# Four 32-wide parts of the array for a linear-attention kernel's state and query products, with weighting in halves and a new written-out order

## The chip, the cores and the metric

The kernel runs on one core of a Trainium2 chip. The metric is the device time of one execution in microseconds (us). Five engines run side by side: TensorE (PE: matmuls; PEld: its weight loads), VectorE (DVE), ScalarE (ACT), GpSimd (POOL), and SyncE (SP), which issues nearly all DMAs.

## What is computed

A transformer block on x of 2048 tokens by 640, in bfloat16: a linear attention with 32 heads of 20 on a layer-normalised x, added to x, then a SiLU feed-forward of width 1728 on the layer-normalised sum, added again. The attention is the part that the change touches:

```python
pq = jnp.einsum("bhsd,hdf->bhsf", q, w_phi)
pk = jnp.einsum("bhsd,hdf->bhsf", k, w_phi)
phi_q = jnp.concatenate([_softmax(pq, axis=-1), _softmax(-pq, axis=-1)], axis=-1)
phi_k = jnp.concatenate([_softmax(pk, axis=-1), _softmax(-pk, axis=-1)], axis=-1)
kv = jnp.einsum("bhsf,bhsd->bhfd", phi_k, v)
z  = jnp.einsum("bhsf->bhf", phi_k)
num = jnp.einsum("bhqf,bhfd->bhqd", phi_q, kv)
den = jnp.einsum("bhqf,bhf->bhq", phi_q, z)[..., None] + 1e-6
o = num / den
```

So each head has a state of 2 x 20 rows (sign s = 0 and 1) by 21 columns (20 of v and one of z), summed over all tokens, and each query row is multiplied with it.

## The kernel before

The 2048 tokens are 16 tiles of 128 rows (t); the 640 channels are 5 chunks of 128 (C). The program has no loop of its own: a string ORDER lists some 630 words, each an operation with its arguments, and every engine executes its part of them in that order, each instruction waiting for what it needs. "kp.3.0.1" is op_kp(3, 0, 1).

The stages, with the words and the lines of what they issue:

- **Weights and inputs.** lx, lk, lv, lp, lq, lo, l1, l2, lh load X, the weights of k, v, the features, q, the output and the feed-forward (nearly all on SP's queue). wt, wc, fk, fc fold the k weights with the feature weights (transposes L303, products L318); lq, gk, gc do it for q. wm (L255) are matmuls on a dummy tile `warm` that warm TensorE up, eight of them ahead of the first word.
- **First normalisation.** st (L261) takes the statistics on VectorE, rs and rm the reciprocal root on POOL, xn (L278 on VectorE or L283 on ACT) the normalised tile, xt and xc or xd (a transposing DMA, L296) its transpose.
- **State.** vp and kp (L348) give v and the features of k; vc copies v beside a column of ones; ke (L369) takes both exponentials, kr (L377, L380) their sums and reciprocals, ka or kb (L385) multiplies them in, on POOL ("p" a whole tile, "h" its first half) and VectorE (kb, the second half). cc (L407) adds a tile's part to the state `kv`, 20 matmuls of all 128 rows by 64 columns of the array: for each sign and chunk, two parts of 64 features stand side by side on the array's columns, each with 4 heads of 21 columns (84). km (L417) multiplies the state with a mask that keeps each head's own block, into KVBD.
- **Queries.** qp (L427) gives the q features of four tiles, qe (L437) the exponentials; dp (L460) multiplies a tile's 128 queries with the state, for each sign in 10 matmuls of 64 rows by 128 columns, with 4 heads of 22 columns (88; the last is z). dw weights the two signs (reciprocal L473, product L474, L476, sum L480), dr (L489) takes the reciprocal of the sum, do (L495, half a tile each, POOL or VectorE) divides, td (L515) transposes by DMA.
- **Output and feed-forward.** op (L522) is the output product, oa (L531) adds X, sq (L539), sa and sr (POOL, L544 to L555), hn (L561) and hd (L581, a transposing DMA) are the second normalisation, up (L596, the tail L606) and ua (L618) the first half of the feed-forward in five groups of 2, 4, 4, 4 and 2 tiles, yp, yq (L642) and yh (L657) the second half, yo and yz (L665, L677) the sum, so and sz the stores.

Nearly all products go through one pool `mm` of four PSUM buffers of two banks. A buffer is free for the next product once all its readers are done; the order of the words decides which product gets which buffer. One buffer holds the state from the first cc to km. dp takes two buffers a tile, one for each sign.

The features of the queries are laid out so that chunk r of the array's rows holds features 64r to 64r + 63 of the first 16 heads in its upper half and of the other 16 in its lower; gc (one copy a chunk) puts Wfq into that layout.

Of the kernel before, what the change touches and what calls it, by code (L numbers as in the profile page):

```python
# [25 lines left out]
lp.a lx.2.4.s ta lk.2.3.s lk.0.1.s mk lk.3.4.s lk.1.2.s lk.4.5.s lv.0.3.s ph.p lx.1.2.s st.3  # L26
lx.0.1.s wt.2 lv.3.5.s st.2 wc.2.a rs.3 lx.4.8.s wm.512 wt.0 wm.256 wt.3 wc.0.a fk.2 wc.3.v rs.2
wt.1 fc.2.a fk.0 xn.3.v fk.3 wc.1.v mc fc.0.a xt.3 fk.1 xc.3.v wt.4 fc.1.a xn.2.v wm.256 vp.3.0.3
lq.4 wc.4.v fc.3.a st.1 mo xt.2 kp.3.0.1 lq.0 xc.2.a kp.3.1.2 kp.3.2.3 st.0 fk.4 vp.2.0.3 fc.4.a
lx.8.12.s rs.0.2 lq.3 vp.3.3.5 kp.3.3.4 vc.3.a kp.3.4.5 xn.0.v vp.2.3.5 lq.1 xn.1.v ke.3 st.5  # L30
kp.2.0.1 kp.2.1.2 xt.0 lh.s kp.2.2.3 st.4 xc.0.a kp.2.3.4 xt.1 vc.2.a kp.2.4.5 lq.2 kp.0 st.6 rs.4.2
ke.2 xn.5.v vp.0 xc.1.a xn.4.v xd.5 st.7 ke.0 kp.1 st.11 lx.12.16.s rs.6.2 vc.0.a xd.4 st.8 vp.1
ke.1 xn.7.v st.10 gk.2 xd.7 gk.0 gc.2.a vp.5 st.9 vc.1.a lo.s gc.0.a kr.1 gk.3 rs.8.4 kp.5 gc.3.a
rm.10 gk.1 xn.9.v ke.5 ka.1.p vp.4 st.12 xd.9 gc.1.a st.14 kp.4 vc.5.a xn.8.v vc.4.a rm.6 st.15 xd.8
vp.7 ke.4 st.13 kp.7 xn.6.a kr.2 rs.12.4 xn.10.a xd.6 vp.9 ke.7 rm.13 xn.12.v ka.2.p kr.4 kp.9 xd.12
vc.9.a vc.7.a gk.4 l2.0.4.s ke.9 vp.8 xd.10 xn.14.v ka.4.p kr.0 gc.4.a vp.6 xn.13.a vc.8.a kr.3 kp.6
rm.11 rm.15 ka.0.p cc.2 kr.7 cc.1 ke.6 cc.4 kp.8 ka.3.p vc.6.a kr.5 xn.15.a qp.0.0 ke.8 xd.15 ka.7.p
kr.9 xd.14 vp.12 qe.0.0 l2.8.13.s ka.5.p kr.8 kp.12 l1.1.s vc.12.a xn.11.a qp.1.0 ke.12 ka.8.p xd.11
kr.12 kp.15 l1.0.s qe.1.0 xd.13 ka.9.p kp.10 l1.2.s l2.4.8.s cc.0 cc.7 ka.12.p ke.10 cc.3 cc.5 cc.8
kr.10 vp.10 kp.14 vc.10.a kr.6 ka.10.p ke.15 kp.11 ke.14 kp.13 ka.6.h ke.11 kr.14 vp.15 ke.13 kr.11  # L40
ka.14.p qp.0.2 qp.0.1 qe.0.2 kr.13 vc.15.a ka.11.p vp.13 kr.15 vp.14 ka.13.p vc.13.a qe.0.1 kb.6
vp.11 vc.14.v ka.15.p cc.12 vc.11.a cc.9 cc.6 cc.11 cc.10 cc.14 cc.13 cc.15 qp.1.2 km.0 close km.1
dp.1.0 qe.1.2 dp.1.1 qp.1.1 dw.1.v dp.0.1 qe.1.1 dp.0.0 dr.1 qp.2.1 dw.0.v dp.3.1 qe.2.1 dp.3.0 dr.0
qp.3.0 dw.3.v do.0.0.p do.0.1.p do.1.1.p td.0 dp.5.0 qe.3.0 dp.5.1 dr.3 qp.2.0 dw.5.v do.3.1.p
do.3.0.p do.1.0.p dp.4.1 td.1 qe.2.0 dp.4.0 op.0 dw.4.v td.3 qp.2.2 oa.0 dp.2.1 qe.2.2 dp.2.0 dr.5
sa.0 qp.3.2 dr.4 dw.2.v do.5.1.p sq.0 op.1 do.5.0.p qe.3.2 sr.0 td.5 dp.9.0 dp.9.1 dr.2 qp.3.1 hn.0
do.2.1.p do.2.0.v hd.0 oa.1 do.4.0.p do.4.1.p dw.9.v sq.1 td.2 op.3 sa.1 qe.3.1 sr.1 td.4 op.5 hn.1
dr.9 hd.1 op.2 oa.5 oa.3 sa.5 op.4 do.9.1.p oa.2 up.0.3 sq.2 oa.4 dp.10.1 sa.4 sq.4 dp.10.0 up.0.0
dw.10.v ua.0.3 sr.4 sq.5 sa.3 do.9.0.p dp.6.0 ua.0.0 dp.6.1 up.0.1 sa.2 dw.6.v td.9 sq.3 sr.3 dp.8.1
# [12 lines left out]
sr.14 yp.6.1 sr.11 hn.14 hn.10 hn.12 hd.10 sr.13 yh.2.1 yh.2.0 hd.12 yp.6.0 so.3 hd.14 yp.9.1 yo.6
hn.13 hd.15 yo.8 yp.7.0 hn.11 hd.11 yp.9.0 hd.13 so.6 up.4.0 so.8 yo.9 up.4.3 up.3.1 ua.4.3 yp.7.1
up.3.0 yo.7 ua.3.1 so.7 ua.4.0 so.2 up.4.1 up.3.3 ua.4.1 up.3.6 ua.3.3 up.4.2 ua.3.6 ua.3.0 up.3.4
ua.4.2 up.3.2 ua.3.4 yp.15.0 ua.3.2 up.3.5 yp.14.0 ua.3.5 yp.15.1 yp.10.0 yh.4.0 yh.3.0 yp.12.1
# [5 lines left out]
def kernel(  # L71
# [613 lines left out]
    with tc.manual_schedule(engines={PE, SP, POOL, DVE, ACT}):  # L685
        ps = None
        for i in range(8):
            ps = op_wm(512, ps)
# [30 lines left out]
```

## Time and profile before

| | us |
|---|---|
| median of 3 runs | 239.42 (239.4 to 240.32) |
| the profiled execution | 240.42 |
| its span, from the first to the last instruction | 238.7 |
| TensorE busy, sum | 232.9 |
| VectorE busy, sum | 136.3 |
| ACT busy, sum | 104.8 |
| POOL busy, sum | 88.8 |

A page and its views name groups of instructions by line, engine, operation and tile. A row of the groups gives the shape, the count, the busy time and the mean length of one, and the idle time ahead of them with what ended most of it. A row of the timeline gives start, length, engine, line and count, and in brackets the idle time before it with its releaser. The chain is the work that ended last, followed back from the last instruction; its rows give start and length of each piece. The stretches give for each window the busy us and counts of PE, PEld, DVE, ACT and POOL, then the granted clock of TensorE, the DMA share and GB/s. Matmuls are pipelined: the length of one reaches past the start of the next, so costs are read from start to start. A few matmul records are missing.

### The profile page before, as it was taken

Reading aid. Unit: us, or ns where it says so; the run is one execution under the profiler, and the core shown is the slowest. Engines: PE = TensorE matmul, PEld = TensorE weight load, DVE = VectorE, ACT = ScalarE, POOL = GpSimd, SP = SyncE. Lnnn points to the kernel's source line nnn. Section 1 sums busy time; section 2 is a strip of 40 time slices with the busy share of each in tenths; the row PEclk is TensorE's granted clock in tenths of the full one; section 3 lists DMA queues with packets and bytes.
Section 4 is the critical chain, followed back from the end, with each engine's and each line's share of the span. In section 5 each row is a group of like instructions: output and inputs, shape, how many; then the busy total and the mean of one; then the engine's idle time right before and its main releaser. Section 6 shows DMA issues by size and latency. Waiting matters only on the chain.

```text
span 238.7 us, 5187 instructions
## 1 busy us (share of the span) xinstructions
PE 232.9 (98%) x2143; PEld 150.8 (63%) x2159; DVE 136.3 (57%) x256; ACT 104.8 (44%) x155; POOL 88.8 (37%) x166
## 2 busy tenths in 40 slices
PE   7999999999999999999999999999999999999994
PEld 3777777577584456787655476664566756656762
DVE  3779999938968999889858139623213120000133
ACT  3678897967545674561043620015660014631000
POOL 5722769998870737464101550001424000000000
PEclk9999999999999999999999999999999999999999
DMA  6997945499000136116480004520103701000013
GB/s 204 314 212 168 233 89 140 87 333 312 4 3 3 27 58 110 31 29 58 84 133 7 17 14 82 110 58 0 29 3 83 156 11 55 0 3 0 26 59 110
DMA packets 42807, 20.60 MB, mean 86 GB/s; under 512 B 34336, under 2 KB 42272, under 8 KB 42784
## 3 DMA queue, kind: packets, MB, share of 16 engines
q1 hardware_dynamic: 41984, 20.11, 36.8%
q8 instruction: 17, 0.28, 0.5%
q10 hardware_dynamic: 800, 0.16, 0.4%
q14 instruction: 6, 0.05, 0.1%
HBM read 9.61 MB, written 2.62 MB: 51 GB/s over the span
## 4 chain that ended last, share of the span: by engine, by line
PE 93%; DVE 2%; DMA 2%; issue 1%; ACT 1%; DVEq 0%
PE mm L596 24%; PE mm L642 21%; PE mm L348 18%; PE mm L427 9%; PE mm L522 9%; PE mm L460 3%; PE mm L407 3%; DMA out_dram<-ob 2%; PE mm L255 2%; PE mm L318 1%; PE mm L606 1%; PE mm L657 1%; ACT EqT L437 1%; PE mm L303 1%; DVE xn L278 1%
## 5 line engine op out<-in xcount | busy, mean ns | idle before, releaser
L618 ACT ACTIVATE shT<-mm 128x1024 bf16<-128x1024 f32 (+2 forms) x29 | 27.5, 963 | 77.9 <-PE mm L596 56.2
L596 PE MATMUL mm<-HnT,w 128*128 128x512 bf16 (+1 forms) x316 | 58.7, 335 | 0.5
L642 PE MATMUL mm<-w,shT 128*128 128x320 bf16 (+2 forms) x415 | 58.5, 299 | 0.2 <-issue 0.2
L642 PEld LDWEIGHTS <-shT 128*128 128x128 bf16 x416 | 39.8, 98 | 17.8 <-issue 1.3
L596 PEld LDWEIGHTS <-w 128*128 128x128 bf16 x325 | 31.2, 98 | 23.1 <-issue 0.4
L665 DVE TENSOR_TENSOR ob<-mm,X 128x640 bf16<-128x640 f32 x15 | 12.2, 822 | 46.7 <-PE mm L642 38.3
L348 PEld LDWEIGHTS <-XnT 128*128 128x128 bf16 x320 | 30.8, 98 | 12.3 <-DMA wv<-in_A_wqkv_dram 0.2
L385 POOL TENSOR_TENSOR Ek<-Ek,Sk 128x1280 bf16<-128x1280 bf16 (+1 forms) x16 | 36.9, 2332 | 2.5 <-DVE Sk L380 1.6
L377 DVE TENSOR_REDUCE Sk<-Ek 128x64 f32<-128x1280 bf16 x16 | 23.1, 1445 | 4.5 <-ACT Ek L369 4.5
L437 ACT ACTIVATE EqT<-mm 128x1024 bf16<-128x1024 f32 (+1 forms) x24 | 19.8, 879 | 11.0 <-PE mm L427 11.0
L348 PE MATMUL mm<-Wfk,XnT 128*128 128x320 bf16 x160 | 24.2, 299 | 0.0
L348 PE MATMUL mm<-wv,XnT 128*128 128x320 bf16 x160 | 24.0, 299 | 0.1
L522 PE MATMUL mm<-wo,ot 128*128 128x320 bf16 x160 | 23.8, 299 | 0.0
L427 PE MATMUL mm<-XnT,Wfq 128*128 128x512 bf16 x94 | 23.1, 380 | 0.4
L495 POOL TENSOR_TENSOR o<-u,rd 128x320 bf16<-128x320 f32 x21 | 15.7, 768 | 20.4 <-DVE rd L489 12.0
L531 DVE SCALAR_TENSOR_TENSOR X<-mm,X 128x640 bf16<-128x640 f32 x16 | 12.9, 815 | 17.2 <-PE mm L522 17.2
L369 ACT ACTIVATE Ek<-mm 128x640 bf16<-128x640 f32 x32 | 20.6, 717 | 4.1 <-PE mm L407 3.0
L522 PEld LDWEIGHTS <-ot 128*128 128x128 bf16 x160 | 15.3, 98 | 7.4 <-issue 0.3
L544 POOL TENSOR_SCALAR HM<-HST 128x1 f32<-128x1 f32 x16 | 3.4, 210 | 40.0 <-DVE X L531 40.0
L427 PEld LDWEIGHTS <-Wfq 128*128 128x128 bf16 x100 | 9.2, 97 | 10.2 <-issue 0.3
L261 DVE BATCH_NORM_STATS2 stats<-X 128x6 f32<-128x320 bf16 x32 | 13.6, 467 | 2.7 <-DMA X<-in_A_x_dram 2.7
L561 DVE TENSOR_SCALAR hn<-X,HM 128x640 bf16<-128x640 bf16 x16 | 7.9, 525 | 12.2 <-POOL HM L555 12.2
(71 smaller groups left out, 212.8 us busy)
## 6 DMA issues: line engine op xcount, KB each, us to landing
out_dram<-ob SPq DMA_DIRECT2D x15, 160.0 KB, 2.0
w<-in_B_w_dram SPq DMA_DIRECT2D x3, 720.0 KB, 6.5
X<-in_A_x_dram SPq DMA_DIRECT2D x3, 640.0 KB, 4.9
w<-in_B_w_dram SPq DMA_DIRECT2D x2, 640.0 KB, 6.0
wk<-in_A_wqkv_dram SPq DMA_DIRECT2D x5, 160.0 KB, 3.4
wo<-in_A_wo_dram SPq DMA_DIRECT2D x1, 800.0 KB, 6.7
w<-in_B_w_dram SPq DMA_DIRECT2D x1, 800.0 KB, 5.3
wv<-in_A_wqkv_dram SPq DMA_DIRECT2D x1, 480.0 KB, 5.8
```

Of the source, the lines that this page charges most:

```text
L261: nc.vector.bn_stats(stats[:, k, :], X[:, t, k * 320 : (k + 1) * 320])
L348: nc.tensor.matmul(ps[:, half, 0:320], tok(XnT[t // GT], t)[:, c, :], W[:, c, half * 320 : (half + 1) * 320], start=(c == 0), stop=(c == C ...
L369: nc.scalar.activation(Ek[:, s, :].rearrange("p (a n) -> p a n", a=2), tl["kp", t][:, :, 0:320], AF.Exp, scale=1.0 - 2.0 * s,)
L377: nc.vector.tensor_reduce(Sk[:], tl["ek", t][:].rearrange("p s (h f) -> p (s h) f", f=DH), axis=AX.X, op=ALU.add,)
L385: eng.tensor_tensor(Ek3, Ek3, tl["sk", t][:, lo:hi].unsqueeze(2).to_broadcast([P, hi - lo, DH]), op=ALU.mult,)
L427: nc.tensor.matmul(ps[:, k, :], Wfq[:, c, r * P : (r + 1) * P], XnT[g][:, c, :], start=(c == 0), stop=(c == C - 1),)
L437: nc.scalar.activation(E[:, s, rs[0] : rs[-1] + 1, :], tl["qp", g, i][:, 0 : len(rs), :], AF.Exp, scale=1.0 - 2.0 * s,)
L495: (nc.vector if eng == "v" else nc.gpsimd).tensor_tensor(tl["o", t][:, a * 320 : (a + 1) * 320].rearrange("p (h f) -> p h f", f=DH), tl["u ...
L522: nc.tensor.matmul(ps[:, half, 0:320], tl["ot", t][:, c, :], wo[:, c, half * 320 : (half + 1) * 320], start=(c == 0), stop=(c == C - 1),)
L596: nc.tensor.matmul(ps[:, i * W : (i + 1) * W], w1[:, c, fc * P : (fc + 1) * P], HnT[g][:, c, 0:W], start=(c == 0), stop=(c == C - 1), skip ...
L618: nc.scalar.activation(sh[:, a:b], tl["up", g, k][:, 0 : b - a], AF.Silu)
L642: nc.tensor.matmul(ps, shT[g][:, fc * W + i * P : fc * W + (i + 1) * P], w2[:, fc, a:b], start=first and fc == 0, stop=last and fc == FC - ...
```

## The change

- **State products (cc).** 40 matmuls a tile in place of 20, each 128 rows by 32 columns of the array: four parts of 32 features stand side by side, part g with heads 8g to 8g + 7, and each covers 3 heads of 21 columns (63) in place of 4 (84).
- **Query products (dp).** One word a tile in place of two; 40 matmuls in place of 20, each 32 rows by 128 columns, with 3 heads of 22 columns (66) in place of 4 (88). The four parts write four PSUM banks: one buffer holds both signs of parts 0 and 1, the other those of parts 2 and 3, so each buffer now holds one half x of the heads.
- **Weighting (dw).** dw.t.x does one half of the heads from one buffer: the same four VectorE instructions twice a tile, on half the elements each.
- **Masks and layout.** op_mc makes its mask with 8 selects on 32 rows and 5 copies on POOL, in place of 4 selects; gc copies twice a chunk; km's shapes are smaller.
- **Warm-up.** `warm` is a constant of ones in place of a tile that VectorE fills; nine matmuls ahead of the first word in place of eight; one wm of 512 columns fewer in the order.
- **Order.** All of ORDER is written anew, for all engines. Some words change engine: xn.6, xn.11, xn.15 to VectorE; kb.10 and kb.15 in place of kb.6; nine of the do words, and some copies. The loads of X, wk and the feed-forward weights stand elsewhere in SP's queue; l2.4.8 and l1.2 now stand between the first output transposes; the two last stores swap queues. The lines move: L409 is the state product in the new file, L463 the query product, L479 to L484 the weighting, L521 the output product, L595 and L641 the feed-forward's.

```diff
-    warm = first.tile([P, 512], BF16, name="warm")
-    nc.vector.memset(warm[:], 0.0)
+    warm = nc.const_aps.tensor(1.0, [P, 512], BF16)
...
-                for a in range(2):
-                    q, lo = C * a + r, 64 * a
+                for g in range(4):
+                    lo, q, h = 32 * g, 160 * g + 32 * r, 8 * g + HW[r]
                     nc.tensor.matmul(
-                        kv[s][lo : lo + 64, r, :, :].rearrange("p j c -> p (j c)"),
-                        Ek[:, s, 64 * q : 64 * q + 64],
-                        Vp[:, HQ[q] : HQ[q] + 4, :].rearrange("p h c -> p (h c)"),
+                        kv[s][lo : lo + 32, r, :, :].rearrange("p j c -> p (j c)"),
+                        Ek[:, s, q : q + 32],
+                        Vp[:, h : h + 3, :].rearrange("p h c -> p (h c)"),
...
+    def op_dp(t):
+        G, i = t // GT, t % GT
+        ps = [mm2(), mm2()]
+        for s in range(2):
+            for r in range(C):
+                for g in range(4):
+                    lo, o = 32 * g, 176 * s + 22 * HW[r]
+                    nc.tensor.matmul(
+                        ps[g // 2][:, g % 2, o : o + 66],
+                        EqT[G][lo : lo + 32, s, r, i * P : (i + 1) * P],
+                        KVBD[lo : lo + 32, s, r, :, :].rearrange("p j c -> p (j c)"),
+                        start=(s == 0 and r == 0),
+                        stop=(s == 1 and r == C - 1),
+                        skip_group_check=True,
+                    )
...
+    def op_dw(t, x):
+        A = tl["dp", t][x]
+        if ("u", t) not in tl:
+            tl["u", t] = wk2().tile([P, 2, 2, 8, 21], F32, name="u", bufs=3)
+        u = tl["u", t][:, x]
+        w = sm.tile([P, 2, 8], F32, name="w")
+        nc.vector.reciprocal(w[:], A[:, :, 1, :, 21])
+        nc.vector.tensor_tensor(w[:], w[:], A[:, :, 0, :, 21], op=ALU.mult)
         nc.vector.tensor_tensor(
-            u[:], A[1][:, :, :, 0:21], w[:].unsqueeze(3).to_broadcast([P, 2, 16, 21]), op=ALU.mult,
-        )
...
+            u, A[:, :, 1, :, 0:21], w[:].unsqueeze(3).to_broadcast([P, 2, 8, 21]), op=ALU.mult,
+        )
+        nc.vector.tensor_tensor(u, u, A[:, :, 0, :, 0:21], op=ALU.add)
...
-        for i in range(8):
+        for i in range(9):
             ps = op_wm(512, ps)
```

The new order from the state's end on, up to the sixth output product:

```
... cc.15 cc.11 qp.1.2 km.0 close km.1 dp.1 qe.1.2 qp.1.1 dw.1.1 dw.1.0 dp.0
qe.1.1 dw.0.1 qp.2.1 dw.0.0 dp.3 qe.2.1 dr.1 qp.2.2 dw.3.1 do.1.1.p do.1.0.p qe.2.2 dr.0 dp.4 td.1
dw.3.0 do.0.1.p qp.3.0 do.0.0.p dw.4.0 td.0 op.1 dw.4.1 l2.4.8.s qe.3.0 dr.3 dp.5 oa.1 do.3.0.p
qp.2.0 dr.4 do.3.1.p sq.1 dw.5.0 sa.1 td.3 sr.1 dw.5.1 op.0 qe.2.0 l1.2.s do.4.1.p do.4.0.p qp.3.2
oa.0 td.4 hn.1 dp.2 qe.3.2 dr.5 qp.3.1 dw.2.1 do.5.1.p hd.1 sq.0 do.5.0.p dw.2.0 sa.0 td.5 sr.0
qe.3.1 op.4 dr.2 hn.0 do.2.1.p do.2.0.v dp.9 oa.4 op.5 td.2 dw.9.1 sa.4 sq.4 hd.0 op.3 dw.9.0 op.2
```

And before:

```
... cc.13 cc.15 qp.1.2 km.0 close km.1
dp.1.0 qe.1.2 dp.1.1 qp.1.1 dw.1.v dp.0.1 qe.1.1 dp.0.0 dr.1 qp.2.1 dw.0.v dp.3.1 qe.2.1 dp.3.0 dr.0
qp.3.0 dw.3.v do.0.0.p do.0.1.p do.1.1.p td.0 dp.5.0 qe.3.0 dp.5.1 dr.3 qp.2.0 dw.5.v do.3.1.p
do.3.0.p do.1.0.p dp.4.1 td.1 qe.2.0 dp.4.0 op.0 dw.4.v td.3 qp.2.2 oa.0 dp.2.1 qe.2.2 dp.2.0 dr.5
sa.0 qp.3.2 dr.4 dw.2.v do.5.1.p sq.0 op.1 do.5.0.p qe.3.2 sr.0 td.5 dp.9.0 dp.9.1 dr.2 qp.3.1 hn.0
do.2.1.p do.2.0.v hd.0 oa.1 do.4.0.p do.4.1.p dw.9.v sq.1 td.2 op.3 sa.1 qe.3.1 sr.1 td.4 op.5 hn.1
dr.9 hd.1 op.2 oa.5 oa.3 sa.5 op.4
```

149 lines of the change are left out of this document (60 added, 89 removed).

## The prediction

> **What bounds the kernel now.** I read the page first: the busy shares, and the engines' shares of the chain of work that ended last.
>
> ```profile
> PE 232.9 (98%) x2143; PEld 150.8 (63%) x2159; DVE 136.3 (57%) x256; ACT 104.8 (44%) x155; POOL 88.8 (37%) x166
> PE 93%; DVE 2%; DMA 2%; issue 1%; ACT 1%; DVEq 0%
> ```
>
> TensorE is busy nearly always, and 93% of the chain is its work. A shorter stream of matmuls shortens the kernel, as long as no other engine takes over. Next, the busy times by stretch (PE, PEld, DVE, ACT, POOL), for the stretches where the change lies.
>
> ```profile
> 60.00:80.00 20.00, 19.84 (x300) 12.06 (x302) 16.36 (x25) 10.43 (x14) 11.12 (x6) 1.00 0.01 2
> 80.00:100.00 20.00, 19.83 (x213) 12.00 (x214) 17.88 (x40) 11.23 (x19) 11.08 (x26) 1.00 0.37 66
> 100.00:120.00 20.00, 19.95 (x219) 14.65 (x218) 18.00 (x35) 5.89 (x9) 8.45 (x22) 1.00 0.36 52
> ```
>
> VectorE is busy 18 of 20 us from 80 to 120: in this stage it is the next bound, close behind TensorE. The change gives it more work just there. That is the core of this forecast.
>
> **What a group of small matmuls costs.** The chain's pieces, then TensorE's timeline (start, length, count).
>
> ```profile
> 46.69 2.16 PE mm L427 x10
> 109.19 5.30 PE mm L642 x39
> ```
>
> ```profile
> 67.73 3.30 PE L407 MATMUL mm<-Vp,Ek 128*64 128x84 bf16 x160
> 70.96 1.25 PE L427 MATMUL mm<-XnT,Wfq 128*128 128x512 bf16 x4
> 72.15 0.57 PE L460 MATMUL mm<-KVBD,EqT 64*128 64x88 bf16 x20
> 72.64 2.33 PE L427 MATMUL mm<-XnT,Wfq 128*128 128x512 bf16 x10
> 74.91 0.57 PE L460 MATMUL mm<-KVBD,EqT 64*128 64x88 bf16 x20
> ```
>
> A whole-array matmul takes 216 ns for 512 columns and 136 ns for 320, so 0.417 ns per column plus 2.7 ns. Ten of them fill 2.16 us from 72.64 to 74.80, and the next group starts at 74.91: entering another shape of the array costs about 0.1 us. Leaving costs as much: 20 small matmuls from 72.15 are followed at 72.64, 0.49 us later. With 0.1 us taken off, ten pairs take 0.39 us, about 40 ns a pair; 80 pairs of L407 take 3.23 - 0.1 us, 39.1 ns a pair. One matmul alone would take 37.7 ns (84 columns) or 39.4 ns (88). So the two halves do run together, and a second part costs at most 1.5 ns.
>
> After the change four parts of 63 (state) or 66 (query) columns stand in place of two. If each added part costs 1.5 ns, a group of four takes 28.9 + 4.5 = 33.4 ns or 30.2 + 4.5 = 34.7 ns; if none does, 29 and 30 ns. I take 33 and 34, the value from the pairs.
> - State products: 160 groups x (39.1 - 33) = **-1.0 us** (bounds -1.6 from 29 ns, and +6.2 from the supply of instructions, below).
> - Query products: 10 groups a tile x (40 - 34) = -0.06 us a tile. The first seven tiles lie in a stretch that I find bound by VectorE and are counted there; nine remain: **-0.5 us** (bounds -0.9 and +3.5).
> - Order: yh.1.0 stands alone, one entry and one leaving more, and dp.7 to yh.0.0 and dp.14 to yh.1.1 are no longer of one shape: **+0.3 us** (0 to +0.4).
>
> The supply is the operation that no row shows. A group of four needs 8 instructions (loads and matmuls) in 33 ns, 4 ns each; in the run of 160 each of 320 came in 9.8 ns. If that were the limit, a group would take 78 ns. The pairs fit their columns so well that I take the columns as what bounds them.
>
> [...]
>
> **Weighting in halves (VectorE).** The groups by shape: count, busy us, mean ns.
>
> ```profile
> L476 DVE TENSOR_TENSOR u<-mm,w 128x672 f32<-128x672 f32 x16 | 13.7, 857 | 1.3 <-ACT EqT L437 0.3
> L480 DVE TENSOR_TENSOR u<-u,mm 128x672 f32<-128x672 f32 x16 | 13.7, 854 | 0.6
> L473 DVE RECIPROCAL w<-mm 128x32 f32<-128x32 f32 x16 | 5.4, 339 | 4.8 <-PE mm L460 4.7
> L474 DVE TENSOR_TENSOR w<-w,mm 128x32 f32<-128x32 f32 x16 | 3.0, 188 | 1.0
> L489 DVE RECIPROCAL rd<-u 128x32 f32<-128x32 f32 x16 | 5.3, 343 | 0.2
> L380 DVE RECIPROCAL Sk<-Sk 128x64 f32<-128x64 f32 x16 | 8.8, 553 | 0.6
> L677 DVE TENSOR_TENSOR ob<-mm,X 128x512 bf16<-128x512 f32 x1 | 0.7, 691 | 1.2 <-DMA out_dram<-ob 1.2
> L677 DVE TENSOR_TENSOR ob<-mm,X 128x128 bf16<-128x128 f32 x1 | 0.3, 292 | 0.0
> ```
>
> The two L677 rows give 1.04 ns per element and 159 ns fixed; for 672 elements that is 858, and the row says 857. A half, 336 elements, takes 508 ns, not 428. A reciprocal costs 6.6 ns per element (553 - 343 over 32): 234 for 16. The small product takes 171. A half is 234 + 171 + 2 x 508 = 1.42 us, a tile 2.84 instead of 2.24: **+0.6 us a tile**, 9.6 us in all (bounds 0, if nothing is fixed, and +0.9, if the gaps between dependent instructions double too). Before 80 us TensorE cannot run far ahead of it, because each tile's two buffers of products stay taken until its halves are weighted, and the buffers are four.
>
> Now VectorE's timeline from the state's end to op.2, the output product that in the new order closes the first six.
>
> ```profile
> 71.08 1.10 DVE L417 TENSOR_TENSOR KVBD<-mm,maskS 128x420 bf16<-128x420 f32 x2 [2.15 <-PE mm L407]
> ...
> 90.04 0.45 DVE L561 TENSOR_SCALAR hn<-X,HM 128x640 bf16<-128x640 bf16 x1
> 90.40 1.02 DVE L495 TENSOR_TENSOR o<-u,rd 128x320 bf16<-128x320 f32 x1
> 91.34 0.81 DVE L531 SCALAR_TENSOR_TENSOR X<-mm,X 128x640 bf16<-128x640 f32 x1
> 92.08 0.08 DVE L531 DVE_READ_ACCUMULATOR X<-mm,X 128x1 f32 x1
> ```
>
> ```profile
> 92.21 5.71 PE L522 MATMUL mm<-wo,ot 128*128 128x320 bf16 x40
> 97.76 0.71 PE L596 MATMUL mm<-HnT,w 128*128 128x256 bf16 x5
> ```
>
> ```profile
> ot<-o SPq DMA_TRANSPOSE x16, 2.6
> ```
>
> Before, do.2.0 (the row at 90.40) ends at 91.42, 20.3 us after L417 began; in it lie dw and dr of six tiles, oa.0 and hn.0. After, the same six tiles stand ahead of it, and oa.1 and hn.1 too (0.74 and 0.36 us from start to start in these rows), and L417 is shorter by 2 x 105 elements x 1.04 = 0.2. That is 20.3 + 6 x 0.6 + 1.1 - 0.2 = 24.8 us. The transpose of tile 2 lands 2.6 us after its issue, which takes some 0.2; op.2 starts at 27.6 and ends 1.36 later, at 29.0. Before, the same TensorE work (seven dp, all qp, six op) ended at 97.76 - 71.08 = 26.7. So TensorE waits here, first for buffers, then for VectorE's last result through POOL and the transpose: **+2.2 us** net of the shorter products (0 to +3.5). Behind op.2 on TensorE stand up.0 and everything later. From there nothing is as tight: VectorE waits for dp.10, the next tile, and catches up.
>
> **Warm-up and start.** The chain's first pieces, the timelines of TensorE and of SP, and one row of the page's DMA issues.
>
> ```profile
> 4.84 0.58 PE mm L303 x5
> ```
>
> ```profile
> 9.64 0.97 PE L348 MATMUL mm<-wv,XnT 128*128 128x320 bf16 x6
> 11.09 0.45 PE L289 MATMUL mm<-ident,xn 128*128 128x128 bf16 x5 [0.48 <-DVE xn L278]
> 11.48 0.97 PE L348 MATMUL mm<-Wfk,XnT 128*128 128x320 bf16 x6
> ```
>
> ```profile
> 3.60 0.44 SPq L221 DMA_DIRECT2D wv<-in_A_wqkv_dram  x1
> 4.21 0.84 SPq L221 DMA_DIRECT2D X<-in_A_x_dram  x2
> ```
>
> ```profile
> wv<-in_A_wqkv_dram SPq DMA_DIRECT2D x1, 480.0 KB, 5.8
> ```
>
> The constant lets TensorE start before VectorE's memset; the ninth warm-up fills that time, so the first transposes stay near 4.8. At 11.48 the old order has done five wt, four fk, two xt and vp.3.0.3, with a wait for xn ahead of the row at 11.09. The new order does both xt before its first vp, which waits for wv: 3.60 + 5.8 = 9.4, plus some 0.4 for the one more X load issued ahead of it. From 9.9, with 6 x 0.136 us, it is as far at 10.7: **-0.8 us** (-1.2 to +0.5). op_mc's 8 selects instead of 4 lie in POOL's wait for the row statistics; uncovered they cost about 2 us to xn.0 and xn.1.
>
> **Normalising, on POOL.** The timeline, then the groups by shape.
>
> ```profile
> 60.53 9.88 POOL L385 TENSOR_TENSOR Ek<-Ek,Sk 128x1280 bf16<-128x1280 bf16 x4 [1.13 <-DVE Sk L380]
> ```
>
> ```profile
> L385 POOL TENSOR_TENSOR Ek<-Ek,Sk 128x1280 bf16<-128x1280 bf16 x15 | 35.6, 2403 | 2.5 <-DVE Sk L380 1.6 <-ACT Vp L163 0.9
> ```
>
> POOL ends at 70.41, just ahead of the last state products (the run from 67.73 to 70.96). The new order gives one more half tile to VectorE (1.1 us less on POOL), but starts POOL after all row statistics. So the state can hardly end 1.8 us earlier, as -0.8 and -1.0 want; I give back **+0.3** (0 to +1.5). xn.6, xn.11, xn.15 and half of tile 15's normalising go to VectorE, five gc copies become ten on ACT; in 60 to 80 these engines have 3.6 and 9.6 us idle (the first stretch above), so I cost them nothing. Without that cover the state ends later, which the +1.5 holds. The last stores change queues behind the last matmul: nothing.
>
> **Sum.** -0.8 - 1.0 + 0.3 + 2.2 - 0.5 + 0.3 = +0.5 us. The profiled execution took 240.4 us (span 238.7, 1.7 around it), so 240.9 in its terms. The median of the runs shown is 239.4, 1.0 less; with the same difference I predict **239.9 us**.
>
> **Rivals.**
> - *Halves are cheap.* If a half costs half, VectorE is done 3.6 us earlier at do.2.0 and op.2 waits for nothing: the stretch goes from +2.2 to -0.4, the time to **237.3**. Against it stands the fixed part in the L677 rows, for it VectorE's 2 us idle in 80 to 100.
> - *Four parts do not run as one (slower side).* [...] At 78 ns, where instructions come no faster than shown, they lose 7.2 + 4.0: **251**. The state's gain turns into a loss at 39 ns. For it: nothing here shows four parts; against: pairs at the pitch of one.
> - *The transposes of o queue behind weights.* l2.4.8 and l1.2 are now issued between td.0 and td.4, instead of before the state's end; the loads' bytes stand in the same queue. If td.4 or td.5 lands 1.5 us later, the op behind it move too: **241.4**.
>
> **How the numbers follow.** The forecast, with its own range 238.4 to 241.0, gets 0.45; cheap halves 0.25; parts that do not run as one 0.17 (0.12 and 0.05); late transposes 0.13. The range is 237.0 to 242.6: it reaches to cheap halves and to 41 ns and leaves out the ends. A measurement tells about 0.5% apart, 238.2 to 240.6. Faster: 0.25 + 0.04 of the forecast, 0.29. Slower: 0.17 + 0.13 and 0.06 of the forecast, 0.36. Same: 0.35.
>
> **What would show it.** In the new profile: groups of L409 and L463 at 33 and 34 ns; halves of L481 and L484 near 508 ns; TensorE idle, or its weight loads waiting for VectorE, between 70 and 100, and op.2 ending 29 us after the first L419; the state's end near 69.5. I am wrong if TensorE shows no wait there, if the halves take 430 ns, or if a group takes over 39 ns.

## The result, and the profile after

The changed kernel takes **254.0 us** (median of 5 runs, 253.4 to 255.3) against 239.5 us before (median of 5, 239.4 to 240.3): a ratio of 1.061, 95% interval 1.057 to 1.064. I had predicted 239.9 (237.0 to 242.6). Of the 14.6 us more, 13.9 stand between the spans of the two profiled executions, 252.6 and 238.7 us. The page of the changed kernel: the busy shares, the chain's shares by engine, and the granted clock.

```profile
PE 235.5 (93%) x2799; PEld 149.9 (59%) x2799; DVE 141.8 (56%) x320; ACT 102.7 (41%) x157; POOL 91.0 (36%) x175
PEclk9999999679999999999999999999999999999999
PE 78%; DVE 9%; issue 5%; DMA 4%; POOL 2%; SPq 1%; ACT 0%; DVEq 0%; POOLq 0%
```

TensorE fell from 98% of the span to 93%, and from 93% of the chain to 78%. Grown on the chain are VectorE (from 2% to 9%) and "issue" (from 1% to 5%): time in which an engine, here TensorE, waited for nothing that the profile shows. And the clock was low once, a fifth of the way in. TensorE's timeline shows where:

```profile
42.15 1.46 PE L409 MATMUL mm<-Vp,Ek 128*32 128x63 bf16 x150
48.38 0.35 PE L409 MATMUL mm<-Vp,Ek 128*32 128x63 bf16 x10 [4.78 <-issue]
48.66 6.59 PE L350 MATMUL mm<-Wfk,XnT 128*128 128x320 bf16 x30
...
58.70 1.54 PE L409 MATMUL mm<-Vp,Ek 128*32 128x63 bf16 x160
60.17 1.53 PE L350 MATMUL mm<-Wfk,XnT 128*128 128x320 bf16 x10
...
74.38 1.78 PE L409 MATMUL mm<-Vp,Ek 128*32 128x63 bf16 x195
78.60 1.20 PE L409 MATMUL mm<-Vp,Ek 128*32 128x63 bf16 x125 [2.44 <-issue]
79.73 0.82 PE L429 MATMUL mm<-XnT,Wfq 128*128 128x512 bf16 x3
82.06 0.61 PE L429 MATMUL mm<-XnT,Wfq 128*128 128x512 bf16 x2 [1.50 <-issue]
82.60 0.49 PE L463 MATMUL mm<-KVBD,EqT 32*128 32x66 bf16 x40
83.02 2.33 PE L429 MATMUL mm<-XnT,Wfq 128*128 128x512 bf16 x10
```

Read the second row from its end. TensorE had done 150 of 160 state products, stopped in the middle of an operation (a tile has 40), stood for 4.78 us, and then did the other 10. It waits for no data: the next ten belong to the same tile. The same happens after 195 products of the last run (2.44 us) and inside the query features behind it (1.50 us). These stops make **8.7 us**. Between the stops the products are fast. The run at 58.70 does 40 groups of four in 60.17 - 58.70 - 0.1 = 1.37 us, 34 ns a group.

Behind the first stop 30 projections took 6.43 us from start to start (48.66 to 55.09); 30 at the 136 ns of before (clock 1.00) are 4.1. The windows (TensorE, loads, VectorE, ScalarE, GpSimd, then the granted clock) give the reason, a clock of 0.50 until about 53.5 us:

```profile
49.00:50.00 1.00, 1.00 (x6) 0.54 (x5) 0.30 (x1) 0.00 (x0) 1.00 (x2) 0.50 0.26 50
54.00:55.00 1.00, 1.00 (x10) 0.73 (x8) 0.00 (x0) 1.00 (x2) 0.00 (x0) 1.00 0.00 0
```

That is **2.4 us** more. The second place is the stretch from the state's end to the first up product. VectorE's first L419, four of TensorE's rows of that stretch, and the window that answers to that of before:

```profile
79.88 0.88 DVE L419 TENSOR_TENSOR KVBD<-mm,maskS 128x315 bf16<-128x315 f32 x2 [4.90 <-PE mm L409]
```

```profile
86.47 2.32 PE L429 MATMUL mm<-XnT,Wfq 128*128 128x512 bf16 x10 [0.69 <-DVE u L484]
...
104.73 1.53 PE L521 MATMUL mm<-wo,ot 128*128 128x320 bf16 x10 [1.15 <-DMA ot<-o]
...
110.24 1.53 PE L521 MATMUL mm<-wo,ot 128*128 128x320 bf16 x10 [0.72 <-DMA ot<-o]
111.61 2.35 PE L595 MATMUL mm<-HnT,w 128*128 128x256 bf16 x20
```

```profile
80.00:100.00 20.00, 17.10 (x272) 8.72 (x271) 16.05 (x49) 10.21 (x14) 6.55 (x13) 1.00 0.28 60
```

TensorE is busy 17.10 of 20 us here, 19.83 before. Of the 2.9 us without work, 1.50 are the third stop; the rest are waits for VectorE and ScalarE, the longest at 86.47 (0.69 us) for a buffer whose half VectorE was still weighting. At 104.73 and 110.24 it waits for transposed tiles (1.15 and 0.72 us). By milestones, in the two profiled executions:

| from ... to | before, us | after, us | more |
|---|---|---|---|
| start to the state's end (first km) | 71.08 | 79.88 | 8.80 |
| state's end to the first up product | 26.68 | 31.73 | 5.05 |
| first up product to the span's end | 140.94 | 140.99 | 0.05 |

The stops are 7.2 us of the first line and 1.5 of the second, the slow clock 2.4 of the first; 3.55 us of the second line are left, and -0.8 us of the first. So the loss is 8.7 + 2.4 + 3.6 - 0.8 = 13.9 us, and all of it lies ahead of the feed-forward.

The -0.8 is hardly a gain of the change. The profiled execution of before took 1.0 us more than the median of its runs, and it lost that at the start: TensorE's first three groups of five transposes took 0.71 to 0.74 us there, those of experiment 4 below 0.44 to 0.45. In the profiles of experiments 4, 6 and 9, whose state products are those of before, the state ends at 70.10, 70.20 and 70.39 us instead of 71.08. The changed kernel without its stops and its slow clock would end it at 79.88 - 7.2 - 2.4 = 70.3. Against these profiles nothing is gained up to there, and 8.7 + 2.4 + 3.6 = 14.7 us stand beside the 14.6 of the medians.

**The reading of the stops.** The page counts DMA packets of the kind "instruction", 16 KB each, on a queue of their own:

```profile
q8 instruction: 22, 0.36, 0.6%
```

22 packets against the 5629 recorded instructions of TensorE (5598 matmuls and loads, and 31 that wait or signal) are one for every 256 (before: 17 and 4327, one for every 255). No view names the engine they serve; by these counts I take them as TensorE's. In the trace TensorE stops behind its 961st, 1985th and 2241st recorded instruction. The differences are 1024 and 256, four times 256 and once: I take these places as the seams of packets. A packet took 1.1, 1.3 and 1.1 us at these three places and TensorE went on 1.3 to 1.6 us after it had landed. The theory: at a seam TensorE can find the next instructions not there yet. 256 instructions of four-part products lasted 256 x 4.2 ns = 1.1 us ahead of the first two stops (the trace has 1.10 and 1.07), while from the start of the seam before to the end of the stop passed 6.1 us (42.30 to 48.38), 3.7 (74.90 to 78.60) and, at the third, from the end of the second, 3.5 (78.60 to 82.05). What sets when a packet comes, and how many instructions lie ready ahead of TensorE, no view shows. The seams cost 8.7 us.

This profile alone does not separate the theory from its rivals: that four parts stop the array by themselves, or that the products wait for what the loads bring. The experiments do.

### The profile page after: what moved, and what is told of

Read it like the earlier page. It is cut to its first block, busy times and chain, and to the rows that moved or that the text cites. A ratio compares the mean times of both kernels' runs of the same rounds, so it can differ in the third digit from the quotient of the medians.

```text
span 252.6 us, 6561 instructions
## 1 busy us (share of the span) xinstructions
PE 235.5 (93%) x2799; PEld 149.9 (59%) x2799; DVE 141.8 (56%) x320; ACT 102.7 (41%) x157; POOL 91.0 (36%) x175
## 4 chain that ended last, share of the span: by engine, by line
PE 78%; DVE 9%; issue 5%; DMA 4%; POOL 2%; SPq 1%; ACT 0%; DVEq 0%; POOLq 0%
PE mm L595 22%; PE mm L641 20%; PE mm L350 18%; PE mm L521 6%; PE mm L429 5%; DMA ot<-o 3%; DVE u L481 2%; PE mm L409 2%; DVE u L484 2%; PE mm L463 2%; DMA X<-in_A_x_dram 2%; PE mm L319 1%; PE mm L605 1%; PE mm L656 1%; POOL o L494 1%
## 5 line engine op out<-in xcount | busy, mean ns | idle before, releaser
L595 PE MATMUL mm<-HnT,w 128*128 128x512 bf16 (+1 forms) x325 | 58.8, 337 | 0.0
L641 PE MATMUL mm<-w,shT 128*128 128x320 bf16 (+2 forms) x416 | 58.4, 299 | 0.0
L617 ACT ACTIVATE shT<-mm 128x1024 bf16<-128x1024 f32 (+2 forms) x29 | 26.8, 963 | 61.6 <-PE mm L595 56.3
L641 PEld LDWEIGHTS <-shT 128*128 128x128 bf16 x416 | 39.7, 98 | 17.6 <-issue 1.6
L595 PEld LDWEIGHTS <-w 128*128 128x128 bf16 x325 | 31.1, 98 | 23.4 <-issue 0.2
L350 PEld LDWEIGHTS <-XnT 128*128 128x128 bf16 x320 | 31.7, 101 | 13.5
L387 POOL TENSOR_TENSOR Ek<-Ek,Sk 128x1280 bf16<-128x1280 bf16 (+1 forms) x16 | 35.9, 2279 | 7.4 <-DVE Sk L382 7.1
L494 POOL TENSOR_TENSOR o<-u,rd 128x320 bf16<-128x320 f32 x24 | 17.9, 763 | 32.8 <-DVE rd L488 17.1
L350 PE MATMUL mm<-Wfk,XnT 128*128 128x320 bf16 x160 | 26.5, 319 | 0.0
L429 PE MATMUL mm<-XnT,Wfq 128*128 128x512 bf16 x100 | 23.7, 379 | 2.6 <-issue 1.5
L521 PE MATMUL mm<-wo,ot 128*128 128x320 bf16 x160 | 23.9, 299 | 2.1 <-DMA ot<-o 2.1
L350 PE MATMUL mm<-wv,XnT 128*128 128x320 bf16 x160 | 23.4, 299 | 0.0
L538 ACT ACTIVATE sq<-X 128x640 bf16<-128x640 bf16 x16 | 11.8, 735 | 23.1 <-DVE X L530 22.4
L521 PEld LDWEIGHTS <-ot 128*128 128x128 bf16 x160 | 15.2, 98 | 9.7 <-DMA ot<-o 3.6
L481 DVE TENSOR_TENSOR u<-mm,w 128x336 f32<-128x336 f32 x32 | 16.2, 507 | 1.7 <-ACT EqT L439 0.3
L484 DVE TENSOR_TENSOR u<-u,mm 128x336 f32<-128x336 f32 x32 | 16.1, 503 | 1.1
```

The costliest lines, as they stand in the source:

```text
L350: nc.tensor.matmul(ps[:, half, 0:320], tok(XnT[t // GT], t)[:, c, :], W[:, c, half * 320 : (half + 1) * 320], start=(c == 0), stop=(c == C ...
L387: eng.tensor_tensor(Ek3, Ek3, tl["sk", t][:, lo:hi].unsqueeze(2).to_broadcast([P, hi - lo, DH]), op=ALU.mult,)
L429: nc.tensor.matmul(ps[:, k, :], Wfq[:, c, r * P : (r + 1) * P], XnT[g][:, c, :], start=(c == 0), stop=(c == C - 1),)
L481: nc.vector.tensor_tensor(u, A[:, :, 1, :, 0:21], w[:].unsqueeze(3).to_broadcast([P, 2, 8, 21]), op=ALU.mult,)
L484: nc.vector.tensor_tensor(u, u, A[:, :, 0, :, 0:21], op=ALU.add)
L494: (nc.vector if eng == "v" else nc.gpsimd).tensor_tensor(tl["o", t][:, a * 320 : (a + 1) * 320].rearrange("p (h f) -> p h f", f=DH), tl["u ...
```

## The experiments

### 1. The seam moved by 126 instructions

```
-        for i in range(9):
-            ps = op_wm(512, ps)
+        for i in range(8):
+            for j in range(9 if i else 8):
+                ps = op_wm(64, ps)
+        ps = op_wm(512, ps)
```

> The changed kernel with 72 short warm-up matmuls in place of 9 long ones: 63 more matmuls and their weight loads, 126 instructions, ahead of everything else; nothing later is touched. Supply theory (TensorE's instructions arrive in packets of 256, and it stands still at its 961st, 1985th and 2241st recorded instruction because a run of four-part products eats a packet faster than the next arrives): the stop inside the first run of state products (4.78 us after its 150th matmul) is gone, one of 2.5 to 4 us appears in the second run of 160 near its 130th matmul, which had none, and the last run stops twice; the clock stays at 1.0 from 48 to 55 us if no stop is over 4 us; 249 to 252 us. Rival (the stop belongs to what the products read or to the loads beside them, not to the count of instructions): 4.8 us at the same matmul of the first run, 254 us.

Measured: 248.1 us, ratio 1.035 (1.031 to 1.039) to before. TensorE's timeline:

```profile
43.15 1.54 PE L409 MATMUL mm<-Vp,Ek 128*32 128x63 bf16 x160
...
52.31 1.31 PE L409 MATMUL mm<-Vp,Ek 128*32 128x63 bf16 x132
54.23 0.39 PE L409 MATMUL mm<-Vp,Ek 128*32 128x63 bf16 x28 [0.61 <-issue]
```

The stop of 4.78 us is gone, and a new one stands in the second run, behind its 132nd product, where 130 was expected. The rival is refuted: same products, same data, same loads, other place. The stop was shorter than expected (0.61 us); its packet was already under way, from 51.61 us, 2.0 us before the stop began. Two things came out otherwise: the last run stopped once (2.33 us), not twice, and the time is below the 249 to 252 us expected. The clock fell to 0.50 at the end of that stop of 2.33 us. The 4 us of the expectation, between the changed kernel's stops of 2.44 us (clock 1.00 behind it) and 4.78 (0.50), did not hold:

```profile
74.00:76.00 2.00, 1.78 (x35) 0.83 (x25) 0.88 (x2) 0.00 (x0) 0.00 (x0) 0.50 0.03 8
```

### 2. The state products spread

In ORDER the 16 cc words move, one to three at a time, between projections (two of the three places are shown; between them cc.2, cc.5, cc.9 and cc.12 move alike):

```
-... ka.2.p cc.6 cc.7 xn.15.v ke.8 cc.4 cc.0 kp.14 ... kp.12 ... kp.10 ... cc.1 kr.14 cc.3 ke.13 cc.2 cc.5 kp.15
+... ka.2.p cc.6 xn.15.v ke.8 kp.14 cc.7 ... kp.12 cc.4 ... kp.10 cc.0 ... cc.1 kr.14 ke.13 kp.15 cc.3
...
-vp.11 vc.15.v kb.15 cc.14 vc.11.a cc.9 cc.8 cc.12 cc.13 cc.10 cc.15 cc.11 qp.1.2 km.0
+vc.14.a cc.14 ka.11.p cc.10 cc.8 vp.11 vc.15.v kb.15 vc.11.a cc.13 cc.15 qp.1.2 cc.11 km.0
```

> The changed kernel with the 16 state products no longer in runs of 4, 4 and 8 tiles but one or two at a time between projections; the same products, as many instructions. Supply theory: the three stops (8.7 us) and the slow clock behind the first (2.4 us) shrink to under 1 us, some nine more runs cost 0.19 us each for the change of array shape, 1.8 us: 244 to 246 us, with the wait for VectorE from 83 to 110 us still there. Rival (four array parts are slow or wait in themselves): the stops stay with the products, 250 us or more.

Measured: 246.9 us (245.5 to 247.6), ratio 1.029 (1.025 to 1.033), 0.9 us above the range expected. Among the waits of its matmuls none for instructions ("issue") is left, and the clock is 1.000 throughout. With as many four-part products as the changed kernel, 7.2 us are gone: four parts are not slow in themselves. The state ends at 72.97 us, 2.7 us later than in the changed kernel without its stops and slow clock (70.3). There are ten more changes of array shape (13 runs instead of 3); at the 0.19 us expected they cost 1.9 us, and where the other 0.8 goes is not shown. The stretch behind it is as in the changed kernel without the 1.5 us stop: 30.2 us, 3.6 more than before.

### 3. The new operations in the old order

> The changed kernel's operations in the order of the kernel before (both halves of a weighting one behind the other, the query products of a tile at the place of the second of the two). Supply theory: no stop in the first two runs of state products, some 2.4 and 1.3 us in and behind the last one, by the count of 256; clock 1.0 throughout; halves of the weighting cost 3.5 us in the stretch up to the sixth output product; products gain 1.4: 239.5 + 3.7 + 3.5 - 1.4 = 245 us. Rival (the new order is what costs, through transposes and loads issued at other places): 239 to 241 us.

The edit is the string ORDER of the kernel before, with "dp.t.1 ... dp.t.0" made one word and "dw.t.v" made "dw.t.0 dw.t.1". Measured: 251.6 us, ratio 1.051 (1.046 to 1.056). The stops came where the theory had them, none in the first two runs, and these:

```profile
67.03 1.77 PE L409 MATMUL mm<-Vp,Ek 128*32 128x63 bf16 x194
70.84 1.20 PE L409 MATMUL mm<-Vp,Ek 128*32 128x63 bf16 x126 [2.04 <-issue]
...
74.57 0.81 PE L429 MATMUL mm<-XnT,Wfq 128*128 128x512 bf16 x3 [2.21 <-issue]
```

The time is over 6 us above what I expected, so the sum was wrong though the stops were right: the stops cost 0.6 more, the halves cost more in this order (first km to the end of the sixth output product 33.1 us, 30.9 without the stop; and 2.4 us more from there to the last matmul). The rest is not accounted for; part of it is clock, which was 1.00 in the profiled execution (250.6 us) and 0.99 to 1.00 in the three others. The rival, that the new order is the fault, is refuted: for these operations the old one is worse behind the state.

### 4. Only the weighting in halves

The kernel before, its products untouched:

```
+        for a in range(2):
+            w = sm.tile([P, 16], F32, name="w")
+            nc.vector.reciprocal(w[:], A[1][:, a, :, 21])
...
+            nc.vector.tensor_tensor(u[:, a], u[:, a], A[0][:, a, :, 0:21], op=ALU.add)
```

> The kernel before, with only the weighting split into two halves of 336 elements, eight VectorE instructions a tile instead of four; products, order and warm-up are untouched. Theory that VectorE is the bound from the state's end to the sixth output product: this stretch grows from 26.7 to about 30 us and the time to about 243 us. My forecast's size of the term was 2.2 us: 241.7. Rival (TensorE's other work hides it): 239.5.

Measured: 248.6 us, ratio 1.037 (1.034 to 1.040). Eight VectorE instructions a tile instead of four, and nothing else, cost 8.9 us, far more than expected (about 243 us in all). Here each half reads both buffers of its tile, so none comes free ahead of the second half; in the changed kernel a half reads one. So 8.9 us is not the price of the halves in the changed kernel. TensorE's timeline at the state's end, where each group of query products and each group behind it now waits for the weighting:

```profile
74.59 0.37 PE L460 MATMUL mm<-KVBD,EqT 64*128 64x88 bf16 x10 [0.29 <-DVE u L477]
75.13 2.32 PE L427 MATMUL mm<-XnT,Wfq 128*128 128x512 bf16 x9 [0.16 <-DVE u L480]
...
77.91 0.37 PE L460 MATMUL mm<-KVBD,EqT 64*128 64x88 bf16 x10 [0.16 <-DVE u L477]
```

From the first km to the end of the sixth output product the kernel needs 31.5 us, 4.7 more than before. Another 3.8 us come later, in an order that was not made for halves; the changed kernel's order loses nothing there (0.05 us in the table above).

### 5. Twice the instructions, no four parts

The kernel before, each state product in two column halves:

```
-                for a in range(2):
+                for b, a in ((0, 0), (0, 1), (1, 0), (1, 1)):
...
-                        Vp[:, HQ[q] : HQ[q] + 4, :].rearrange("p h c -> p (h c)"),
+                        Vp[:, HQ[q] + 2 * b : HQ[q] + 2 * b + 2, :].rearrange("p h c -> p (h c)"),
```

> The kernel before, with each state product cut into two matmuls of half the columns (42 instead of 84): two parts of the array as before, twice as many instructions, the same work; nothing else is touched. Supply theory (the count of instructions in dense runs is what stops TensorE, whatever the parts): one stop of about 2 us in the last run of state products near its 985th matmul and one of about 1 us 128 matmuls later, 242 to 243 us. Rival (running four parts at once is what stops it): no stop, 239.7 us.

Measured: 248.0 us, ratio 1.034 (1.032 to 1.037); 242 to 243 were expected.

```profile
69.51 3.33 PE L407 MATMUL mm<-Vp,Ek 128*64 128x42 bf16 x198
73.50 2.12 PE L407 MATMUL mm<-Vp,Ek 128*64 128x42 bf16 x122 [0.66 <-issue]
...
77.50 0.56 PE L460 MATMUL mm<-KVBD,EqT 64*128 64x88 bf16 x19 [0.56 <-issue]
```

Two stops at the expected places, with two parts of the array: the count of instructions makes them, not the four parts. They are short, 0.66 and 0.56 us, and these products are slower than I took them: 198 in 3.33 us are 32 ns a pair of 42 columns, not 20, so 256 instructions, 64 pairs, last 2 us, not 1.3. The slower products alone explain most of the 4.6 us by which the state ends later. Another 3.4 us come far behind the stops, from waits of about 1 us such as this one:

```profile
104.26 0.71 PE L596 MATMUL mm<-HnT,w 128*128 128x256 bf16 x5 [1.01 <-DVE X L531]
```

Two things had just ended when this up product started: the sum X that the row names (at 104.11 us), and the transpose of its tile (landed at 104.13). The trace does not tell which of the two it had waited for, but the transpose was long. This is the DMA view from its issue (100.1 us) to the product's start:

```profile
q8 instruction: 1, 0.02, 1.5%
issues: line engine op xcount, KB each, median us to landing
HnT<-hn SPq DMA_TRANSPOSE x1, 4.0
```

4.0 us instead of 2.6, with a packet of instructions in the same window. Experiment 9 takes this up.

### 6. Only the warm-up from the constant

```
-    warm = first.tile([P, 512], BF16, name="warm")
-    nc.vector.memset(warm[:], 0.0)
+    warm = nc.const_aps.tensor(1.0, [P, 512], BF16)
```

and nine warm-up matmuls instead of eight.

> The kernel before, with only the warm-up changed: nine matmuls on the constant instead of eight on a tile that VectorE clears. My forecast put the whole new start at 0.8 us gained, most of it by the order. Theory now: the first projection waits for the weight wv and for the normalised tiles, not for the warm-up: 239.5 us, within 0.3. Rival (the earlier clock brings the whole stream forward): 238.7 us.

Measured: 240.0 us, ratio 1.0004 (0.9987 to 1.0021). It does nothing that can be measured.

### 7. The loads out of the way

Two words of ORDER move: "l2.8.13.s" and "lo.s" from ahead of the first cc to behind the last.

> The changed kernel with the loads of wo and of one part of the second weight (800 and 800 KB) issued behind the state's end instead of shortly before the first state products; TensorE's stream is the same. Theory that the first stop is long (4.8 us, the others 2.4 and 1.5) because the packet of instructions queues behind these loads: the first stop falls to 2.0 to 2.8 us, the clock stays at 1.0 behind it, and 249 to 250 us. Rival (a packet takes that long anyway): 4.8 us and 254.

Measured: 251.0 us, ratio 1.048 (1.045 to 1.051), 3 us less than the changed kernel.

```profile
42.07 1.46 PE L409 MATMUL mm<-Vp,Ek 128*32 128x63 bf16 x150
45.79 0.27 PE L409 MATMUL mm<-Vp,Ek 128*32 128x63 bf16 x10 [2.25 <-issue]
45.99 4.25 PE L350 MATMUL mm<-Wfk,XnT 128*128 128x320 bf16 x30
```

Same matmul, half the stop, and the projections behind it run at full clock (30 in 4.25 us). The packet came at 43.15 us, in the changed kernel at 45.66. So the loads made the first stop long; its place is set by the count. Only 3 of the 4.9 us (2.5 of stop, 2.4 of clock) came back, and 249 to 250 us were expected: the later stops took 2.34 and 2.05 us here (2.44 and 1.50 in the changed kernel), and behind them the clock fell (0.62 from 78 to 80 us, 0.53 from 80 to 82).

All stops together show the pattern. Counted by 256 from the first stop, the seams lie behind the recorded instructions 705, 961, 1217, 1473, 1729, 1985 and 2241. TensorE stopped, to within five records (a few of matmuls are missing), at 1473 and 2241 in experiment 1, at 1985 and 2241 in experiments 3 and 5, and at 961, 1985 and 2241 in experiment 7. Ahead of each of these stops, the seam before it lies in a dense run, so nearly all of the 256 instructions between the two are small products. In the changed kernel the first run holds the seams 705 and 961 and stops at the second; the second run holds 1217 alone and does not stop. In the kernel before, no run of state products holds two. One seam does not fit: the last run of experiment 1 holds 1729 and 1985 and did not stop at 1985; a packet had come from 67.03 to 68.20 us there, before that run began.

### 8. VectorE relieved, twice

First, in the kernel of experiment 2, by moving the sum of one half of each of the first six tiles away:

```
+        if first and t in (0, 1, 2, 3, 4, 5):
+            up = wk2().tile([P, 2, 8, 21], F32, name="up", bufs=2)
+            nc.scalar.copy(up[:], A[:, :, 0, :, 0:21])
+            nc.gpsimd.tensor_tensor(u, u, up[:], op=ALU.add)
```

> The kernel with the spread state products (second experiment) and, for the first six tiles, the last addition of one half (0.50 us on VectorE) moved away: ScalarE copies the products out and GpSimd adds. Theory that VectorE is the bound from the state's end to the sixth output product: 6 x 0.5 = 3 us less VectorE work there, the stretch shrinks from 30.4 to 27.5 or 28 us and the time by 2.5 us, to about 244.3. Rival (the stretch is as long as the buffers of products and the transposes make it): 30 us and 247.

Measured: 249.6 us, ratio 1.041 (1.038 to 1.043): slower, not faster. GpSimd's timeline, then TensorE's:

```profile
82.85 0.90 POOL L488 TENSOR_TENSOR u<-u,up 128x336 f32<-128x336 f32 x1 [1.97 <-ACT up L487]
83.70 2.78 POOL L500 TENSOR_TENSOR o<-u,rd 128x320 bf16<-128x320 f32 x4
```

```profile
87.75 1.53 PE L527 MATMUL mm<-wo,ot 128*128 128x320 bf16 x10 [1.62 <-DMA ot<-o]
```

In experiment 2 GpSimd began the first o at 81.03 us; here the addition of a later tile stands ahead of it in the queue, and every transpose and output product moves back (1.1 us of that because the state ended later in this execution). The edit took one wait away and made another, so it decides nothing about VectorE. The second try therefore leaves that addition out and puts nothing in its place:

```
-        nc.vector.tensor_tensor(u, u, A[:, :, 0, :, 0:21], op=ALU.add)
+        if not (first and t in (0, 1, 2, 3, 4, 5)):
+            nc.vector.tensor_tensor(u, u, A[:, :, 0, :, 0:21], op=ALU.add)
```

> The kernel with the spread state products (second experiment), with the last addition of one half left out in the first six tiles and nothing put in its place: 6 x 0.50 us less on VectorE, no other engine gets more. (The sum over the two signs is then missing in these halves.) Theory that VectorE is the bound from the state's end to the sixth output product: the stretch shrinks from 30.4 to about 27.5 us and the time from 246.9 to about 244. Rival (buffers of products and transposes set it, as moving the addition to GpSimd seemed to say): 30 us and 247.

Measured: 244.4 us, ratio 1.020 (1.017 to 1.023), 2.4 us less than experiment 2 by the medians and 1.2 by the profiled executions. The windows from 80 to 100 us of experiment 2 and of this one, and the last output product of the six here:

```profile
80.00:100.00 20.00, 17.29 (x278) 9.70 (x272) 17.76 (x52) 12.15 (x18) 10.77 (x23) 1.00 0.61 131
```

```profile
80.00:100.00 20.00, 18.15 (x267) 10.05 (x252) 16.73 (x51) 11.93 (x18) 10.70 (x23) 1.00 0.72 130
```

```profile
100.67 1.53 PE L523 MATMUL mm<-wo,ot 128*128 128x320 bf16 x10 [0.93 <-DMA ot<-o]
```

The stretch went from 30.4 to 28.9 us: half of the 3 us that were taken off VectorE. VectorE does bound it, but not alone. What holds the other half is not tested; TensorE still waits 0.46 and 0.93 us for transposed tiles there.

### 9. Transposes and packets of instructions

In the profile of before, five of the 32 transposes that were issued after 80 us took more than 2.75 us, and the same five overlap with a packet of instructions on q8. In the changed kernel and in experiments 2, 4 and 5 nearly all long ones have a packet of instructions (q8 or the other queue of that kind, q14) beside them, or a big load just ahead. To test it, the kernel before with 112 more instructions at the front (the edit is that of experiment 1, with 64 short matmuls for 8 long ones):

> The kernel before, with 64 short warm-up matmuls in place of 8 long ones: 56 more matmuls, 112 instructions, ahead of everything; all else untouched. Theory that a transposing DMA takes 2.6 us alone and 2.8 to 5.2 us when a packet of TensorE's instructions lands beside it: the transposes at 88.8, 108.5, 110.0, 122.9 and 156.0 us, the only ones over 2.75 us, come down to 2.6, and ones near 83, 95, 149 and 186 us, which took 2.6, take 2.8 us or more, since the packets now fall there; the time moves by up to 1 us either way, 239 to 241.5. Rival (those transposes are long for what they carry or where they stand): the same five stay long.

Measured: 241.9 us, ratio 1.010 (1.006 to 1.013). The DMA view of before from 108 to 112.7 us, and the same transposes in the shifted kernel:

```profile
q8 instruction: 1, 0.02, 1.9%
issues: line engine op xcount, KB each, median us to landing
HnT<-hn SPq DMA_TRANSPOSE x2, 3.8
```

```profile
q1 hardware_dynamic: 1344, 0.33, 40.8%
issues: line engine op xcount, KB each, median us to landing
HnT<-hn SPq DMA_TRANSPOSE x2, 2.6
```

No packet, and the two come down from 3.8 to 2.6 us. All five did (2.57 to 2.63). Near 149 and 186 us the packets now fall beside other transposes, and five of these went from 2.6 to 3.0 to 4.4 us. The two places nearer 83 and 95 us changed little (2.7) or not at all, since the packets came beside the transposes' ends or later than I had reckoned. So here these transposes were long by where the packets fell, and lines of code far ahead decided that. How much of the 1.0% is theirs isn't separated: the other warm-up (64 matmuls in 3.93 us, 8 in 3.59 before) is in it too, and the profiled execution, the fastest of the five, does not show it (its span is 238.8 us, that of before 238.7).

## Why the prediction was wrong, step by step

- **What a group of four costs: right in size, the reason not shown.** Predicted 33 and 34 ns; 34 ns (state, above) and, from the rows at 82.60 and 83.02, (0.42 - 0.1) / 10 = 32 ns (query). But 66 columns took less than 63, which columns plus 1.5 ns a part do not give, and the pairs of experiment 5 took 32 ns where 42 columns, by the 0.417 ns each plus 2.7 of the prediction, give 20. Groups of 42, 63 and 66 columns all took 32 to 34 ns; what sets that is not shown, and the match may be luck. No run shows the 41 ns a group that the range reaches to and that has 0.12 of the chances: the groups of four took 34 and 32 ns.
- **The supply of instructions: the step that failed.** I asked how fast instructions come and took 9.8 ns from a run that had kept up; priced it as 78 ns a group, all along, at 251 us; and gave it 0.05, because "the pairs fit their columns so well that I take the columns as what bounds them". The pairs do fit. But in these runs supply is no rate that every matmul feels. It shows at the seams of 256 instructions: where the 256 ahead of one were nearly all small products, 1.1 us of four parts or 2 of the split pairs, TensorE stopped at all but one of the seams listed in experiment 7; in the changed kernel 3.5 to 6.1 us passed from the seam before to the end of a stop. That a delivery takes so long is my reading of these stops; no run shows it by itself. In the kernel before no run of pairs held two seams; as the longest has 320 instructions, that was in part luck. Cutting each product in two doubled the instructions of a run while its time stayed nearly the same, and TensorE stopped. The time of 254 lies near the 251 of that rival, but for another reason: 8.7 us of stops at three seams, which experiments 1, 2, 5 and 7 moved, removed, made and shortened.
- **The clock: not thought of.** I took 1.00 throughout. The stop of 4.78 us had a second price: 6.8 us at 0.50, which cost 2.4 us.
- **Weighting in halves: the instructions right in size, what hangs on them too small.** The halves take what I said:

```profile
L481 DVE TENSOR_TENSOR u<-mm,w 128x336 f32<-128x336 f32 x32 | 16.2, 507 | 1.7 <-ACT EqT L439 0.3
L484 DVE TENSOR_TENSOR u<-u,mm 128x336 f32<-128x336 f32 x32 | 16.1, 503 | 1.1
```

  508 was predicted. In experiment 2, where no stop blurs it, do.2.0 ends 24.2 us after the first L419 (24.8 predicted). But op.2 ends 30.4 us after it, not 29.0: the transpose of that tile took 4.4 us, beside a packet of instructions, where I took 2.6 from the median. The term was 3.55 us instead of 2.2, just past its bound of 3.5. How much of it the halves make, and how much the late transposes of the new order, is not separated: taking 3 us off VectorE gave half of that back (experiment 8).
- **"From there nothing is as tight": right** in the new order (0.05 us from the first up product on, -0.2 predicted with the products' gain and the order's changes). In the old order it would have been wrong (experiments 3 and 4).
- **Warm-up and start: wrong, no gain.** Six vp are done at 11.09 us in the changed kernel, not at 10.7, and at 11.48 in the profile of before. But that profile is the one with the slow start: experiments 3 to 6 and 9, which start in the old order, are there at 9.97 to 10.75 us, and experiments 1, 2, 7 and 8, which start in the new one, at 10.41 to 11.42. So the -0.8 was a comparison with one slow execution. The constant itself gains nothing (experiment 6).
- **The state's end: too early.** With -0.8, -1.0 and +0.3 it was to come 1.5 us earlier, near 69.5. Without the stops and the slow clock it comes at 70.3, as in experiments 4, 6 and 9. The products do gain, by the rows 160 x (39.1 - 34) = 0.8 us; the start takes back about 0.5 (the mean of the times above), and the rest is not traced.
- **GpSimd's normalising (+0.3):** hidden behind the stops, not tested.
- **Late transposes** were a rival at 241.4 because of weights in the queue. Two (4.3 and 3.6 us) stood behind a load as described, and TensorE waited 1.15 us for the first of them (at 104.73); but the end of the stretch is set by the transpose of tile 2 behind it. The other long ones stood beside packets of instructions, which I did not have.

Still open is what sets when a packet comes, and a variant with four parts and one weighting per tile wasn't tried. No version here beats the kernel before.

## What to carry to other kernels

Count instructions as well as columns: here 256 matmuls and loads of four-part products lasted 1.1 us, and TensorE stopped for 8.7 us at three seams of 256. With the same products spread between projections it had none of these stops (experiment 2), and with 1.6 MB of loads moved away the longest fell from 4.78 to 2.25 us (experiment 7). So try long matmuls between runs of short ones, and keep big loads away from such runs. Look at what splits along with a product: two halves of a VectorE instruction here cost more than the four parts gained. When a wait is removed by giving its work to another engine, look first at what stands in that engine's queue.

## What the runs showed of the hardware

- TensorE stopped at places that lie multiples of 256 recorded instructions apart, to within five records, in five kernels. Eleven stops lasted 0.56 to 2.44 us, and in the longest of them (changed kernel, 76.1 to 78.6 us) no DMA packet started; the twelfth lasted 4.78 us beside 1.6 MB of loads.
- In and after a stop of 4.8 us the granted clock was 0.50 for 6.8 us, at one of 2.3 us (experiment 1) for 3.4; the stops of 2.4 and 1.5 us in the changed kernel, and of 2.0 and 2.2 us in the profile of experiment 3, left it at 1.00. So the length of a stop alone does not decide it.
- A transposing DMA issued behind the state took 2.56 to 2.7 us alone and up to 5.2 us (changed kernel) with packets of instructions beside it.
- Pairs of 64-wide parts started every 32 ns with 42 columns (experiment 5) and every 39 ns with 84 (before): half the columns saved a fifth of the time.
